# Three of twelve streamed weight blocks loaded in two DMAs each, over 12 and 8 engines

## The chip, the cores and the metric

The kernel runs on one core of a Trainium2 chip (trn2). The metric is the device time in microseconds (us) of one execution. All times are of whole executions of the same program, of which the profile shows one.

## The reference

Two computations share nothing but the output: `a` fills the first 1024 columns, `b` the last 1024. Part A is an attention over 64 segments of 32 rows, one after the other, each with a memory of 8 rows that is the first part of the segment before's output:

```
for s in range(n_seg):                        # 64 segments of 32 rows, Dm = 1024
    h = concatenate([mem, x[s]])              # 8 + 32 rows
    q, k, v = h @ Wq, h @ Wk, h @ Wv          # 32 heads of 128: weights 1024 x 4096 each
    p = softmax(where(mask, q k^T * scale, -1e9))
    o = (p v) @ Wo                            # 4096 x 1024
    mem = o[:, :8]
    outs.append(o[:, 8:])
```

Part B is a state space convolution: a kernel K (from A, B, C and log_dt, 1024 channels of 128 states) is convolved with u over 2048 steps, and `u * Dskip` is added.

## The kernel before, in words

**Order of the stages.** Part B runs first, to about 620 us. In its gaps, part A's weights are loaded and everything of the projections that doesn't depend on the memory is computed ahead and put into DRAM (`PKd`, `VXd`). From about 640 to 1893 us the segment loop of part A runs (`part_a`, the loop over `s` at L406), one segment after the other, since each needs the memory that the one before leaves. A last stage up to 1954 us computes the output rows that were put off (from `OLd`).

**The weights.** Each segment multiplies a small matrix (`a_hT`, 32 columns) by all the weights: 64 blocks of 128 x 2048 bf16, 512 KB each. A block is named by its matrix, half and index, such as (v, 0, 7), here written v07; a block of the output projection by its index, such as o8. 52 blocks stay on the chip all the time, in SBUF and partly in PSUM. Twelve do not fit and are loaded anew in each segment: `STREAM` (L26) and `STREAM_O` (L27) list them. In order of use they are k02, q02, k11, k15, q14, v02, v07, v14, v17, o4, o8, o13.

**How they are streamed.** `streamed_copies` (L63) makes a copy of each of the twelve in DRAM, `WD_...`, of 128 x 2048 in one piece, so that a row is 4096 bytes without a gap. That happens once, during part B. In the loop, `unit` (L300) returns the tile for a block; for a streamed one it calls `stage` (L337), which takes the next of four SBUF slots in turn (`SLOTS = 4`, the tiles `wst` with tags w0 to w3) and issues one DMA on SP's queue (L340). The three first streamed blocks are loaded ahead of the loop (`first`, L1707), and one of the output projection once more behind it (L647).

**What sets the order.** The loop is written under a manual schedule (L290): every engine works through its instructions in the order of the code. A load may start when PE has used the block that was in the slot four loads before; SP waits for that, and what stands behind it on SP waits too. PE uses a block as soon as it has landed: the matmuls of q, k and v are at L414, those of the output projection at L527.

**The other DMAs of a segment** are issued by ACT: `PKd` (L376, 128 KB, the prepared keys), the store to `OLd` (L392), the store of output rows (L396) and the load from `VXd` (L382). GpSimd's copy at L428 waits for `PKd`.

**Semaphores of DMAs.** The DMAs issued by SP and ACT take eight completion semaphores in turn, in the order of the program. A DMA that takes a semaphore waits until the DMA that had it before, eight places back, has landed.

Of the kernel before, what the change touches and what calls it, by code (L numbers as in the profile page):

```python
# [10 lines left out]
BF16 = mybir.dt.bfloat16  # L11
# [13 lines left out]

STREAM = {("k", 0): (2,), ("q", 0): (2,), ("k", 1): (1, 5), ("q", 1): (4,), ("v", 0): (2, 7), ("v", 1): (4, 7)}  # L26
STREAM_O = (4, 8, 13)  # L27

BANK = {("k", 0): "b0", ("q", 0): "b1", ("k", 1): "b2", ("q", 1): "b0", ("v", 0): "b3", ("v", 1): "b2"}
KEPT = {("k", 0, 7): (("K7a", 0, 512), ("K7b", 512, 512), ("K7c", 1024, 512), ("K7d", 1536, 384), (None, 1920, 128)),  # L30
# [28 lines left out]
def streamed_keys():  # L59
    return [key for key in [(m, t, kc) for (m, t), kcs in STREAM.items() for kc in kcs] + [("o", u) for u in STREAM_O]]  # L60


def streamed_copies(ctx, tc, src):  # L63
    nc = tc.nc
    dram = ctx.enter_context(tc.tile_pool(name="a_wd", bufs=1, space=bass.MemoryType.DRAM))
    out, copies = {}, []
    for key in streamed_keys():
        t_ = dram.tile([128, 2048], BF16, name="WD_%s" % "_".join(str(i) for i in key))
        copies.append(lambda t_=t_, key=key: nc.sync.dma_start(
            out=t_[:].rearrange("e (h d) -> e h d", h=2) if key[0] == "o" else t_[:], in_=src(key)))  # L70
        out[key] = t_
    return out, copies


class Ahead:
# [3 lines left out]
    def __init__(self, ctx, tc, x, src, seg_len):  # L79
        self.nc, self.tc, self.x, self.src = tc.nc, tc, x, src  # L80
        self.S, self.Dm = x.shape
        self.SL, self.XM = seg_len, 24
        self.XL, self.KC, self.NS = seg_len - 24, self.Dm // 128, self.S // seg_len
        dram = ctx.enter_context(tc.tile_pool(name="a_dram", bufs=1, space=bass.MemoryType.DRAM))
        self.VXd = dram.tile([self.NS + 1, 128, 256 + self.KC * self.XM], BF16, name="VXd")
        self.PKd = dram.tile([self.NS, 128, 512], BF16, name="PKd")
        self.PVd = [dram.tile([self.NS * self.XL, 2048], BF16, name="PVd%d" % t) for t in range(2)]
        self.OLd = dram.tile([self.NS // 8, 128, 8 * 256], BF16, name="OLd")
# [183 lines left out]
def part_a(ctx, tc, x, src, WD, HE, seg_len, out_a, ahead, W_res, rest, places, first):  # L272
    nc = tc.nc
# [26 lines left out]
    def unit(key):  # L300
        if key in rest:

            rest.remove(key)
            load_resident(tc, wres, src, key, W_res, None, places.pop(0)() if places else None)
        if key in W_res:
            return W_res[key]
        if key in KEPT:
            return ahead_of.pop(key) + halves.get(key, [])
        between.pop(key, lambda: None)()
        if key in first:  # L310
            return first.pop(key)
        if key[0] == "v":
            for k_ in rest[0:3 if key[1] == 0 else 1]:
                rest.remove(k_)
                load_resident(tc, wres, src, k_, W_res)
        return stage(key, WD[key][:])

    ctx_l = ctx_w.enter_context(ExitStack())
    pers = ctx_l.enter_context(tc.tile_pool(name="a_pers", bufs=1))
# [14 lines left out]
    def words(out, in_):  # L334
        nc.vector.tensor_scalar(out=out.bitcast(I32), in0=in_.bitcast(I32), scalar1=0, scalar2=None, op0=ALU.bitwise_or)  # L335

    def stage(key, in_):  # L337
        t_ = wst.tile([128, 2048], BF16, name="wst", tag="w%d" % (loads[0] % SLOTS))
        loads[0] += 1
        nc.sync.dma_start(out=t_[:].rearrange("e (h d) -> e h d", h=2) if len(in_.shape) == 3 else t_[:], in_=in_)  # L340
        return t_

    def load_kept(key):
# [62 lines left out]
    for s in range(NS):  # L406
# [123 lines left out]
        a = quads("k", 0, (0, 2, 4, 6, 1, 3, 5, 7))  # L530
        k0 = evac(a, "k0")
        a = quads("q", 0, range(0, 6))
# [4 lines left out]
        a = quads("k", 1, range(0, 3))  # L537
# [16 lines left out]
        a = quads("q", 1, range(KC))  # L554
# [3 lines left out]
        a = quads("v", 0, range(0, 3))  # L558
# [34 lines left out]
        a = quads("v", 1, range(0, 5))  # L593
# [46 lines left out]
    wo = {}  # L640
    for u in order:
        if ("o", u) in W_res:
            wo[u] = W_res["o", u]
        else:
            wo[u] = spare.pop(0)
            if ("o", u) in WD:
                nc.sync.dma_start(out=wo[u][:], in_=WD["o", u][:])  # L647
            else:
                nc.sync.dma_start(out=wo[u][:].rearrange("e (h d) -> e h d", h=2), in_=src(("o", u)))
    stores(NS - 1, ob)  # L650
# [6 lines left out]
    for b in range(4):  # L657
        pe = [ps_k.tile([128, 512], F32, name="pe", tag="keep%d" % (2 * (b % 2) + n)) for n in range(2)]
        for u in order:
            for hh in range(2):  # L660
                h = 2 * u + hh
                hi = 16 * (h // 16) + 4 * (h % 4) + (h % 16) // 4
# [983 lines left out]
@with_exitstack  # L1646
def kernel(
    ctx: ExitStack,
    tc: tile.TileContext,
    A_x: bass.AP,  # L1650
    A_mem0: bass.AP,
    A_Wq: bass.AP,
    A_Wk: bass.AP,
    A_Wv: bass.AP,
    A_Wo: bass.AP,
    A_seg_len: bass.AP,
    B_u: bass.AP,
    B_A_re: bass.AP,
    B_A_im: bass.AP,
    B_B_re: bass.AP,  # L1660
    B_B_im: bass.AP,
    B_C_re: bass.AP,
    B_C_im: bass.AP,
    B_log_dt: bass.AP,
    B_Dskip: bass.AP,
    out: bass.AP,
):
    seg_len = int(A_seg_len)
    Dm = A_x.shape[2]
    Db = B_u.shape[2]  # L1670
    out_a = out[0, :, 0:Dm]
    out_b = out[0, :, Dm:Dm + Db]
    src = weight_blocks(A_Wq.rearrange("d h e -> d (h e)"), A_Wk.rearrange("d h e -> d (h e)"),
                        A_Wv.rearrange("d h e -> d (h e)"), A_Wo.rearrange("h e d -> (h e) d"))
    WD, copies = streamed_copies(ctx, tc, src)
    ahead = Ahead(ctx, tc, A_x[0], src, seg_len)
    ctx_w = ctx.enter_context(ExitStack())
    W_res, places, first = {}, [], {}
    rest = Keys(RESIDENT)
    rest.ctx = ahead.ctx = ctx_w  # L1680

    def residents(stay, early, uqs, last):
        def put(t_):
            load_resident(tc, None, src, rest.pop(0), W_res, None, t_)
        for _ in range(EARLY[0]):
            load_resident(tc, stay, src, rest.pop(0), W_res)
            yield
        def some(where, tag, n):
            t_ = where.tile([128, n, 2048], BF16, name="W%d" % n, tag=tag)
            return [t_[:, i, :] for i in range(n)]  # L1690
        for t_ in some(stay, "KT1", 2):
            put(t_)
            yield
        for t_ in early:
            put(t_)
            yield
        put(last[0])
        yield
        for t_ in uqs:
            put(t_)  # L1700
            yield
        ahead.wst = ctx_w.enter_context(tc.tile_pool(name="a_wst", bufs=1, side="right"))
        pool = ctx_w.enter_context(tc.tile_pool(name="a_wre0", bufs=1, side="right"))
        for _ in range(EARLY[1]):
            load_resident(tc, pool, src, rest.pop(0), W_res)
            yield
        for i, key in enumerate([("k", 0, 7)] + streamed_keys()[0:SLOTS - 1]):  # L1707
            first[key] = t_ = ahead.wst.tile([128, 2048], BF16, name="wst", tag="w%d" % i)
            tc.nc.sync.dma_start(out=t_[:], in_=WD[key][:] if key in WD else src(key))
            yield  # L1710
        for i in [c // 2 for c in PAIRS]:
            places.append(lambda i=i: stay.tile([128, 2048], BF16, name="W1", tag="MI%d" % i))
        for i in range(LATE):
            put(places.pop(0)())
            yield
        put(last[1])
        yield

    low = low_blocks(ctx, tc)
    ahead.low = low.pop()  # L1720
    copies += [lambda t_=t_: load_resident(tc, None, src, rest.pop(0), W_res, None, t_) for t_ in low]

    def first_state(m0, xt):
        nc = tc.nc
        consts = constants(tc, ahead)
        hT = next(consts)
        nc.sync.dma_start(out=xt[:].rearrange("p k r -> p (k r)"), in_=ahead.VXd[0, :, 256:])
        nc.sync.dma_start(out=m0, in_=A_mem0[0])
        pm = yield
        for kc in range(8):  # L1730
            nc.tensor.transpose(out=pm[:, kc, :], in_=m0[:, kc * 128:(kc + 1) * 128], identity=ahead.consts[0][0:8, 0:8])
        nc.vector.tensor_copy(out=hT[:, :, ahead.XM:], in_=pm)
        nc.gpsimd.tensor_copy(out=hT[:, :, 0:ahead.XM], in_=xt[:])
        yield
        next(consts)
        yield

    with ExitStack() as ctx_b:
        part_b(ctx_b, tc, B_u[0], B_A_re, B_A_im, B_B_re, B_B_im, B_C_re, B_C_im, B_log_dt, B_Dskip, out_b, ahead, copies, residents, first_state)
    with ExitStack() as ctx_a:  # L1740
        part_a(ctx_a, tc, A_x[0], src, WD, A_Wo.shape[0] * A_Wo.shape[1], seg_len, out_a, ahead, W_res, rest, places, first)
# [35 lines left out]
```

## Time and profile before

| what | value |
|---|---|
| runs | 1960.46, 1957.11, 1960.54 us, median 1960.46 us |
| profiled execution: span | 1954.2 us, 2.9 to 6.3 us under the runs |
| PE busy | 1810.2 us (93%) |
| VectorE (DVE) busy | 1379.4 us (71%) |
| ScalarE (ACT) busy | 934.7 us (48%) |
| GpSimd (POOL) busy | 443.1 us (23%) |
| mean granted TensorE clock | 0.974 |
| DMA queue with the most bytes (q1, SP's) | 531.85 MB, 79.9% of 16 engines' span |

The span runs from the first to the last instruction. For the profiled execution no time but the span is given; the runs are timed separately. PE is the matrix engine, PEld its loading of the stationary operand, SPq and ACTq the queues from which SP and ACT issue DMAs. `wst<-WD_v` is a streamed block of v loaded into a slot. A wait line reads: engine, line, what it produces, what it waited for, then the total in us, how often, and the longest.

### The profile page before, as it was taken

Reading aid. Unit: us, or ns where it says so; the run is one execution under the profiler, and the core shown is the slowest. Engines: PE = TensorE matmul, PEld = TensorE weight load, DVE = VectorE, ACT = ScalarE, POOL = GpSimd, SP = SyncE. Lnnn points to the kernel's source line nnn. Section 1 sums busy time; section 2 is a strip of 40 time slices with the busy share of each in tenths; the row PEclk is TensorE's granted clock in tenths of the full one; section 3 lists DMA queues with packets and bytes.
Section 4 is the critical chain, followed back from the end, with each engine's and each line's share of the span. In section 5 each row is a group of like instructions: output and inputs, shape, how many; then the busy total and the mean of one; then the engine's idle time right before and its main releaser. Section 6 shows DMA issues by size and latency. Waiting matters only on the chain.

```text
span 1954.2 us, 74192 instructions
## 1 busy us (share of the span) xinstructions
PE 1810.2 (93%) x31750; PEld 1106.9 (57%) x31788; DVE 1379.4 (71%) x3431; ACT 934.7 (48%) x1670; POOL 443.1 (23%) x855
## 2 busy tenths in 40 slices
PE   8999999887997899999999999999999999998998
PEld 3666666556775555555555555555555555555554
DVE  8599989889994566666676766676766676666650
ACT  8799989851122334344434443444444444444320
POOL 2364545223222111111111111111111111111120
PEclk8999999878998999999999999999999999999999
DMA  7889898867589999999999999999999999999991
GB/s 222 243 232 283 237 287 243 221 188 253 169 272 334 347 340 340 340 339 336 355 339 346 345 335 336 339 341 350 344 350 334 347 341 347 339 350 324 338 343 30
DMA packets 337342, 591.08 MB, mean 302 GB/s; under 512 B 94848, under 2 KB 211048, under 8 KB 334964
## 3 DMA queue, kind: packets, MB, share of 16 engines
q1 hardware_dynamic: 284824, 531.85, 79.9%
q10 hardware_dynamic: 45532, 29.57, 4.9%
q0 software_dynamic: 6656, 24.92, 3.5%
q8 instruction: 249, 4.08, 0.8%
q14 instruction: 81, 0.66, 0.1%
HBM read 528.78 MB, written 68.47 MB: 306 GB/s over the span
## 4 chain that ended last, share of the span: by engine, by line
PE 37%; DMA 27%; DVE 4%; issue 1%; ACT 1%; POOL 0%; SPq 0%; ACTq 0%; DVEq 0%; POOLq 0%
PE acc L414 20%; DMA wst<-WD_v 8%; PE pp L527 8%; DMA wst<-WD_o 7%; DMA wst<-WD_k 3%; DMA arena<-PKd 3%; DMA wst<-WD_q 3%; PE pe L664 3%; PE tr L425 2%; DMA out_dram<-arena 1%; DMA out_dram<-uu 1%; PE pv L495 1%; PE pv L499 1%; DVE arena L621 1%; PE sc L439 1%
## 5 line engine op out<-in xcount | busy, mean ns | idle before, releaser
L414 PEld LDWEIGHTS <-a_hT 128*32 128x32 bf16 x12352 | 328.4, 96 | 324.0 <-issue 64.0
L420 ACT CAST arena<-acc 128x512 bf16<-128x512 f32 x384 | 224.8, 585 | 404.3 <-PE acc L414 324.5
L414 PE MATMUL acc<-wst,a_hT 128*32 128x512 bf16 x2304 | 229.5, 382 | 34.2 <-DMA wst<-WD_v 22.9
L527 PEld LDWEIGHTS <-arena 128*32 128x32 bf16 x8256 | 216.1, 96 | 73.2 <-issue 49.3
L335 DVE TENSOR_SCALAR arena<-keep 128x256 int32<-128x256 int32 (+1 forms) x512 | 175.6, 395 | 28.1 <-PE acc L414 28.0
L428 POOL COPY arena<-arena 128x128 bf16<-128x128 bf16 x128 | 37.3, 292 | 683.0 <-DMA arena<-PKd 314.4
L414 PE MATMUL acc<-XM,a_hT 128*32 128x512 bf16 x2560 | 172.7, 380 | 0.0
L458 ACT ACTIVATE sc<-sc 128x160 f32<-128x160 f32 (+1 forms) x192 | 63.9, 333 | 127.6 <-DVE sc L455 127.6
L454 DVE TENSOR_REDUCE a_mx<-sc 128x4 f32<-128x160 f32 (+1 forms) x192 | 71.7, 374 | 74.7 <-PE sc L442 73.3
L197 PE MATMUL pro<-XM,wsl 128*128 128x512 bf16 x480 | 117.7, 383 | 5.3 <-DVE kst L206 2.2
L527 PE MATMUL pp<-W_o,arena 128*32 128x256 bf16 x3584 | 120.6, 273 | 0.1
L414 PE MATMUL acc<-W,a_hT 128*32 128x512 bf16 x1536 | 120.0, 384 | 0.0
L542 DVE COPY arena<-tr 128x512 bf16<-128x512 bf16 x64 | 27.2, 425 | 128.8 <-PE tr L425 128.8
L462 DVE TENSOR_REDUCE a_mx<-sc 128x4 f32<-128x160 f32 (+1 forms) x192 | 72.9, 379 | 55.3 <-ACT sc L458 54.9
L489 POOL TENSOR_TENSOR arena<-arena,a_BD 128x128 bf16<-128x128 bf16 x128 | 51.1, 399 | 231.1 <-DVE arena L472 229.7
L1266 DVE TENSOR_SCALAR nr<-ptt 128x456 f32<-128x456 int16 x128 | 80.4, 628 | 31.8 <-PE ptt L1244 29.0
L1258 ACT ACTIVATE E<-pa 128x648 bf16<-128x648 f32 x128 | 87.7, 712 | 18.1 <-PE pa L1250 16.0
L414 PE MATMUL acc<-wq,a_hT 128*32 128x512 bf16 x1024 | 92.2, 381 | 0.0
L414 PE MATMUL acc<-g,a_hT 128*32 128x512 bf16 x1024 | 90.4, 379 | 0.0
L1459 POOL TENSOR_TENSOR Bt<-ev 128x512 bf16<-128x512 f32 x32 | 55.7, 1760 | 150.2 <-DVE ev L1456 150.2
L621 ACT CAST arena<-pp 128x128 bf16<-128x128 f32 x64 | 17.0, 265 | 149.8 <-DVE arena L621 149.8
L425 PEld LDWEIGHTS <-arena 128*128 128x128 bf16 x1024 | 57.8, 98 | 54.4 <-issue 45.1
(339 smaller groups left out, 4071.3 us busy)
## 6 DMA issues: line engine op xcount, KB each, us to landing
wst<-WD_v SPq DMA_DIRECT2D x256, 512.0 KB
wst<-WD_k SPq DMA_DIRECT2D x192, 512.0 KB
wst<-WD_o SPq DMA_DIRECT2D x192, 512.0 KB
wst<-WD_q SPq DMA_DIRECT2D x128, 512.0 KB
Ud<-ux POOLq DMA_DIRECT2D x16, 1024.0 KB, 8.2
wq<-Ud SPq DMA_DIRECT2D x32, 512.0 KB
wsl<-in_A_Wk_dram SPq DMA_DIRECT2D x16, 512.0 KB
wsl<-in_A_Wv_dram SPq DMA_DIRECT2D x16, 512.0 KB
```

The source lines that it names most:

```text
L197: nc.tensor.matmul(a[:], lhsT=w[:, kc, 128 * j:128 * j + 128], rhs=xTl[:, kc, :, :].rearrange("p s k -> p (s k)"), start=(kc == 0), stop=( ...
L335: nc.vector.tensor_scalar(out=out.bitcast(I32), in0=in_.bitcast(I32), scalar1=0, scalar2=None, op0=ALU.bitwise_or)
L414: nc.tensor.matmul(a[32 * g:32 * g + 32, o_:o_ + rhs.shape[1]], lhsT=hT[:, kc, :], rhs=rhs, start=(kc == 0), stop=(kc == KC - 1), tile_pos ...
L420: nc.scalar.copy(out=q, in_=a[:])
L425: nc.tensor.transpose(out=p[:, hl, :, :].rearrange("p a b -> p (a b)"), in_=q[:, 128 * hl:128 * hl + 128], identity=ident[:])
L454: nc.vector.tensor_reduce(out=m_, in_=x, axis=AX.X, op=ALU.max)
L458: nc.scalar.activation(out=flat(sc, i), in_=flat(sc, i), func=ACT.Exp, scale=scale)
L462: nc.vector.tensor_reduce(out=m_, in_=x, axis=AX.X, op=ALU.add)
L527: nc.tensor.matmul(po[32 * qt:32 * qt + 32, o_:o_ + rhs.shape[1]], lhsT=oT[:, h % 4, (h % 16) // 4, :], rhs=rhs, start=False, stop=(h == 3 ...
L664: nc.tensor.matmul(pe[n][:], lhsT=left[2 * b + hi // 16][:, 128 * (hi % 16):128 * (hi % 16) + 128], rhs=wo[u][:, 1024 * hh + 512 * n:1024 ...
L1258: sc.activation(out=T["E", r, e // 4][:, lo:lo + 8 * NE].rearrange("p (i c) -> p i c", i=2), in_=T.pop(("p", r, e))[:, :, 0:4 * NE], func= ...
L1266: v.tensor_scalar(out=T["n", r, e // 4][:, lo:lo + 8 * NT], in0=T.pop(("t", r, e))[:, 0:8 * NT].bitcast(I16)[:, 0:16 * NT:2], scalar1=floa ...
```

## The change

The list `PORTIONS` names three of the twelve streamed blocks: k15, v07 and o8. Each is stored in DRAM in two parts and loaded by two DMAs. The first part has 120 rows, stored as 12 stretches of 10 rows; between stretches 64 elements (128 bytes, `PITCH`) are left free, so the 12 stays an outer dimension of the access pattern. The second part has 8 rows, stored as 8 stretches of one row. The slot in SBUF stays one tile of 128 x 2048: rows 0 to 119 come from the first DMA, rows 120 to 127 from the second, which follows it at once on SP's queue. The copies into DRAM are split in the same way. The other nine blocks are loaded as before. A new class `Streamed` holds the parts, makes the copies and issues the loads (in the changed kernel the issue stands at L98).

```diff
@@ -25,6 +25,7 @@
 
 STREAM = {("k", 0): (2,), ("q", 0): (2,), ("k", 1): (1, 5), ("q", 1): (4,), ("v", 0): (2, 7), ("v", 1): (4, 7)}
 STREAM_O = (4, 8, 13)
+PORTIONS = {key: ((120, 12), (8, 8)) for key in (("k", 1, 5), ("v", 0, 7), ("o", 8))}
 
 BANK = {("k", 0): "b0", ("q", 0): "b1", ("k", 1): "b2", ("q", 1): "b0", ("v", 0): "b3", ("v", 1): "b2"}
 KEPT = {("k", 0, 7): (("K7a", 0, 512), ("K7b", 512, 512), ("K7c", 1024, 512), ("K7d", 1536, 384), (None, 1920, 128)),
@@ -60,16 +61,47 @@
     return [key for key in [(m, t, kc) for (m, t), kcs in STREAM.items() for kc in kcs] + [("o", u) for u in STREAM_O]]
 
 
+PITCH = 64
+
+
+class Streamed:
+
+    def __init__(self, dram, nc, src, key):
+        self.nc, self.src, self.key, self.pieces = nc, src, key, []
+        lo = 0
+        for i, (rows, engines) in enumerate(PORTIONS.get(key, ((128, 16),))):
+            name = "WD_%s_%d" % ("_".join(str(j) for j in key), i)
+            each = rows // engines
+            if key in PORTIONS:
+                t_ = dram.tile([engines, each * 2048 + PITCH], BF16, name=name)
+                ap = t_[:, 0:each * 2048].rearrange("a (b f) -> a b f", f=2048)
+            else:
+                ap = dram.tile([128, 2048], BF16, name=name)[:]
+            self.pieces.append((lo, lo + rows, ap))
+            lo += rows
+        assert lo == 128
+
+    def copy(self):
+        for lo, hi, ap in self.pieces:
+            flat = ap if len(ap.shape) == 2 else None
+            w = self.src(self.key)[lo:hi]
+            if self.key[0] == "o":
+                w = w.rearrange("(a b) h d -> a b h d", a=ap.shape[0]) if flat is None else w
+                out = ap.rearrange("a b (h d) -> a b h d", h=2) if flat is None else ap.rearrange("e (h d) -> e h d", h=2)
+            else:
+                w = w.rearrange("(a b) f -> a b f", a=ap.shape[0]) if flat is None else w
+                out = ap
+            self.nc.sync.dma_start(out=out, in_=w)
+
+    def load(self, t_):
+        for lo, hi, ap in self.pieces:
+            self.nc.sync.dma_start(out=t_[lo:hi, :], in_=ap)
+
+
 def streamed_copies(ctx, tc, src):
-    nc = tc.nc
     dram = ctx.enter_context(tc.tile_pool(name="a_wd", bufs=1, space=bass.MemoryType.DRAM))
-    out, copies = {}, []
-    for key in streamed_keys():
-        t_ = dram.tile([128, 2048], BF16, name="WD_%s" % "_".join(str(i) for i in key))
-        copies.append(lambda t_=t_, key=key: nc.sync.dma_start(
-            out=t_[:].rearrange("e (h d) -> e h d", h=2) if key[0] == "o" else t_[:], in_=src(key)))
-        out[key] = t_
-    return out, copies
+    out = {key: Streamed(dram, tc.nc, src, key) for key in streamed_keys()}
+    return out, [w.copy for w in out.values()]
 
 
 class Ahead:
@@ -313,7 +345,7 @@
             for k_ in rest[0:3 if key[1] == 0 else 1]:
                 rest.remove(k_)
                 load_resident(tc, wres, src, k_, W_res)
-        return stage(key, WD[key][:])
+        return stage(key)
 
     ctx_l = ctx_w.enter_context(ExitStack())
     pers = ctx_l.enter_context(tc.tile_pool(name="a_pers", bufs=1))
@@ -334,10 +366,10 @@
     def words(out, in_):
         nc.vector.tensor_scalar(out=out.bitcast(I32), in0=in_.bitcast(I32), scalar1=0, scalar2=None, op0=ALU.bitwise_or)
 
-    def stage(key, in_):
+    def stage(key):
         t_ = wst.tile([128, 2048], BF16, name="wst", tag="w%d" % (loads[0] % SLOTS))
         loads[0] += 1
-        nc.sync.dma_start(out=t_[:].rearrange("e (h d) -> e h d", h=2) if len(in_.shape) == 3 else t_[:], in_=in_)
+        WD[key].load(t_)
         return t_
 
     def load_kept(key):
@@ -644,7 +676,7 @@
         else:
             wo[u] = spare.pop(0)
             if ("o", u) in WD:
-                nc.sync.dma_start(out=wo[u][:], in_=WD["o", u][:])
+                WD["o", u].load(wo[u])
             else:
                 nc.sync.dma_start(out=wo[u][:].rearrange("e (h d) -> e h d", h=2), in_=src(("o", u)))
     stores(NS - 1, ob)
@@ -1706,7 +1738,10 @@
             yield
         for i, key in enumerate([("k", 0, 7)] + streamed_keys()[0:SLOTS - 1]):
             first[key] = t_ = ahead.wst.tile([128, 2048], BF16, name="wst", tag="w%d" % i)
-            tc.nc.sync.dma_start(out=t_[:], in_=WD[key][:] if key in WD else src(key))
+            if key in WD:
+                WD[key].load(t_)
+            else:
+                tc.nc.sync.dma_start(out=t_[:], in_=src(key))
             yield
         for i in [c // 2 for c in PAIRS]:
             places.append(lambda i=i: stay.tile([128, 2048], BF16, name="W1", tag="MI%d" % i))
```

## The prediction

> **What bounds the kernel now.** I began with the page's head and slices, went on to the windows, then to the waits of PE and SP, and last to the timeline of one segment. 0.2% (4 us) is about what a measurement of this kernel can tell from no change.
>
> ```profile
> span 1954.2 us, 74192 instructions
> PE   8999999887997899999999999999999999998998
> DMA  7889898867589999999999999999999999999991
> q1 hardware_dynamic: 284824, 531.85, 79.9%
> q10 hardware_dynamic: 45532, 29.57, 4.9%
> q8 instruction: 249, 4.08, 0.8%
> PE acc L414 20%; DMA wst<-WD_v 8%; PE pp L527 8%; DMA wst<-WD_o 7%; DMA wst<-WD_k 3%; DMA arena<-PKd 3%; DMA wst<-WD_q 3%; PE pe L664 3%; PE tr L425 2%; DMA out_dram<-arena 1%; DMA out_dram<-uu 1%; PE pv L495 1%; PE pv L499 1%; DVE arena L621 1%; PE sc L439 1%
> ```
>
> From slice 13 on, PE and the DMA engines are both at 9 tenths: the segment loop, about 640 to 1893 us. The streamed blocks (WD_) are most of what DMA adds to the chain that ended last. The window of the loop (us, PE, PEld, DVE, ACT and POOL busy, clock, DMA share, GB/s):
>
> ```profile
> 640.00:1893.00 1253.00, 1187.82 (x25440) 693.37 (x25430) 832.09 (x2603) 518.64 (x1140) 200.20 (x510) 1.00 0.96 342
> ```
>
> TensorE has its full clock, PE is busy for 95%, the 16 DMA engines for 96%. A segment lasts 19.60 us (median spacing of PKd's issue). So there is little spare on either side, and what is lost in a segment comes 63 times. What PE waits for in this window (us, times, longest), and SP's and POOL's largest waits:
>
> ```profile
> PE acc L414 <- DMA wst<-WD_v: 16.5, 23, 2.4
> PE pp L527 <- DMA wst<-WD_o: 8.8, 18, 1.3
> PE acc L414 <- DMA wst<-WD_k: 6.4, 11, 1.1
> PE acc L414 <- DMA wst<-WD_q: 4.3, 6, 0.9
> SPq L340 <- PE acc L414: 337.4, 375, 1.6
> POOL arena L428 <- DMA arena<-PKd: 314.4, 48, 8.3
> ```
>
> Only 36.0 us of PE's time goes to late blocks, 0.57 us a segment; SP itself mostly waits for PE to free a slot. One segment's timeline (start, length, what):
>
> ```profile
> 1101.23 0.33 ACTq L376 DMA_DIRECT2D arena<-PKd  x1
> 1101.90 0.62 ACTq L392 DMA_DIRECT2D OLd<-arena  x1
> 1102.56 0.55 ACTq L396 DMA_DIRECT2D out_dram<-arena  x1
> 1106.32 0.32 SPq L340 DMA_DIRECT2D wst<-WD_v  x1
> 1112.14 0.39 PE L414 MATMUL acc<-wst,a_hT 128*32 128x512 bf16 x4
> ```
>
> The fourth line is v07 (block v, 0, 7), the fifth its first use. By the trace's semaphore records PKd landed at 1107.34, OLd at 1108.82, out_dram at 1108.12, v07 at 1111.21, 0.93 us before its use. Over all segments the slack (first use less last landing) has median 0.51 us for v07 (mean 0.53, tenths 0.09 and 0.89), 0.49 (mean 0.54) for k15, 0.31 (mean 0.34) for o8.
>
> **The change, part by part.** Everything is summed against the span, 1954.2 us. The runs shown lie 2.9 to 6.3 us above it, their median 6.3, and that is added at the end.
>
> *Instructions.* PE, DVE, ACT and POOL keep theirs in their order. SP gets 3 more DMAs for the copies, 3 in nearly every one of the 64 segments, and one in the last reload, 196 in all. An issue takes 0.32 us on SP. In the loop these fit into the 337 us and more that SP waits for PE, so I take nothing; uncovered, 192 x 0.32 = 61 us. Ahead of the loop the copies carry the same bytes: 0, within 5 us either way.
>
> *The waits that move (first term).* In the program of both kernels the DMAs of SP and ACT take eight completion semaphores in turn, and each waits until the DMA eight places before it has landed. Before, a segment has 12 on SP and 4 on ACT, 16 in all, so each block always follows the same older DMA: v17 follows PKd, o4 OLd, o13 out_dram, the next k11 VXd, and these had landed 2.5, 3.0, 5.7 and 6.6 us (medians) before the issue. After, there are 19, and the partners move: v07's first piece waits for this segment's PKd, its second piece for OLd, v17 for out_dram, o13 for VXd. In the trace of before, v07 is issued a median 0.91 us before PKd lands and 1.77 us before OLd lands (in 98% and 100% of the segments), v17 0.89 us after out_dram's landing, o13 2.05 us after VXd's. So only v07 is held: its 8-partition piece goes out 1.77 us later. Behind it on SP's queue stand v14 (issued 0.23 us before OLd's landing, so put back by 0.5 with the issues ahead), then v17; v14's wait is in the same stall and is not added. The small piece queues behind the same older packets, so I let it land 1.35 us later than the whole block did. The lower bound is 0.9 (as if only PKd's landing counted), the upper 1.8. Against a slack of 0.53 that scatters, PE stalls 0.85 us a segment (1.35 less 0.53, and a little for the segments that have no slack): 63 x 0.85 = 53 us. The bounds give 63 x (0.9 less 0.53) = 23 and 63 x (1.8 less 0.53) = 80.
>
> *The spread over engines (second term).* A 4096-byte packet takes 159 ns (median) and 180 ns (mean) in 700 to 1850 us. A whole block is 8 packets on each of 16 engines. Split, it is 10 on twelve and one more on eight: 11 on engines 0 to 7, 10 on the next four, none on the last four. That is 3 x 0.18 = 0.54 us later on the busiest engines, if the engine numbers go up from zero; that the first lists really use 12 and 8 engines can be read from stores of these shapes elsewhere in the trace, which land in 12 and 8 parts. For k15 and o8 this takes the slack: with scatter about 0.17 and 0.24 us a segment, 63 x 0.41 = 26 us; between 0 (if the last lander is on an engine that is skipped) and 63 x 1.08 = 68 (no slack at all).
>
> The other nine blocks have to pass engines 0 to 7, which carry 105 packets a segment and not 96, 9 x 0.18 = 1.6 us. With a share of 0.96 they are busy for 18.8 of 19.6 us, so they would need 20.4: a floor of 0.8 us a segment, 63 x 0.8 = 50 us, if packets keep their mean time. This is not added to the stall of v07: both stretch the same segment, and the longer one covers the other. I take half a term on top of the 79, as it bites in bursts: +15, between 0 and 50.
>
> *Relief.* PE stalled at v07 lets v14, v17 and o4, next in line, land in time; their gaps are now 0.16, 0.05 and 0.05 us: 63 x 0.26 = 16, of which I take back 13. The last four engines carry 24 packets less; a quarter of the 36 us of waits, 9 us, could go with them. Sum: 53 + 26 + 15 - 13 - 9 = +72.
>
> *Partitions (third term).* [...] Loads of 8 rows over 8 engines in 295.5 to 301 us had a median packet of 202 ns and not 159 (12 packets); in 305.8 to 313 us they were at 159. So 0 to 11 x 43 ns = 0.47 us for a split block, 0 to 63 x 3 x 0.47 = 89 us if none of it hides. I take 0, since only one of two rows shows it, and keep the end for the range.
>
> [...]
>
> 1954.2 + 72 = 2026, with 6.3 for the runs 2032.
>
> **The rivals.**
>
> *A: the skipped engines were the late ones (faster).* A block's sixteenth landing comes 0.5 to 0.6 us after the fifteenth, the others 0.1 apart. PE's own instruction fetches (q8; 16 KB, 0.92 to 1.06 us, 3.1 in a segment) hold one engine each. If that engine is mostly among the last four, a split block lands 0.5 us sooner, and the 8 packets fewer on each late engine pull the rest along. Price: a gain of 20 to 36 of the 36 us, at worst less 6 for a rest of v07's wait: 1960.5 less 14 to 36 is 1924 to 1946. It decides if most last landings are there and v07's slack absorbs OLd's landing. Against: the packet after a fetch shows a pattern with period 8 over successive fetches, which speaks for a rotation over eight engines, and the slack is 0.53 against 1.35. Chance 0.10.
>
> *B: v07's wait is mostly covered.* A longer segment drains the queues, PKd and OLd land earlier, and the 8-row piece overtakes. Then v07 costs 0.1 to 0.2 us and the spread's 26 us is left, with relief of 9: +25 to +35, 1985 to 1996. For: every lost 0.3 us eases the queue. Chance 0.20.
>
> *C: engines 0 to 7 become the bound.* The floor of 50 us holds, with the partition term on top (a third to all of 89): +80 to +140, 2040 to 2100. For: 0.96 leaves no room. Chance 0.22.
>
> *D: the spread doesn't happen* (the lists merge back into 16 engines). Then only the moved waits stay: 53 less 13, with the relief of none: 2000. The gap of 128 bytes between the parts in DRAM speaks against it. Chance 0.05. No change at all, from terms that cancel: 0.03.
>
> **How the numbers follow.** The forecast of 2032 (its own range 2005 to 2060) has 0.40. With A 0.10, B 0.20, C 0.22, D 0.05 and 0.03 for no change, the range from 1978 to 2100 leaves out A, no change and C's far end. Slower by over 0.2%: 0.87; faster: 0.10; same: 0.03.
>
> **What would show it.** Right: PE's waits for WD_v rise from 16.5 to some 60 us, at v07; SP waits for OLd and PKd at the load's line; segments last 20.6 to 20.8 us; the DMA share of the window falls, as the last four engines idle. For A, segments are under 19.4 us and all four wait rows shrink. For B, WD_v stays under 30 and WD_k and WD_o grow. For C, all rows grow and split blocks' packets are longer than 180 ns. Wrong in its first step, if v07's second piece is issued at once after the first.

## The result, and the profile after

The changed kernel takes 2212.41 us (median of four runs, 2207.93 to 2215.60) and the kernel before 1960.50 us on the same chip: 1.129 times the time, with a 95% interval from 1.126 to 1.131. The change costs 252 us, or 4.0 us in each of 63 segments. The forecast had the sign, with 72 us instead of 252.

From the page of the kernel after: span, the slices of PE and of DMA, the queue of SP, and the chain that ended last.

```profile
span 2212.9 us, 74490 instructions
PE   8999998879867787887887887878778887888789
DMA  7889987685899999989989989999999999998992
q1 hardware_dynamic: 285608, 531.85, 78.2%
DMA wst<-WD_o 15%; DMA wst<-WD_v 14%; DMA wst<-WD_k 9%; PE pp L559 6%; PE acc L446 5%; DMA OLd<-arena 5%; DMA arena<-PKd 4%; PE pe L696 2%; SPq L98 1%; DMA out_dram<-arena 1%; DVE arena L497 1%; DVE arena L503 1%; DVE a_mx L494 1%; DVE arena L545 1%; DMA out_dram<-uu 0%
```

Up to slice 12 the two kernels look alike; in the loop PE falls from 9 to 7 or 8 tenths, while DMA stays at 8 or 9. The bytes of q1 are the same. In the chain, streamed blocks of v, o, k and q were 21% before; now v, o and k alone are 38%. The stretch of the loop that was shown of before (it holds 53 segments of this kernel, and 63 of the kernel before):

```profile
640.00:1893.00 1253.00, 1011.18 (x21100) 581.38 (x21104) 688.49 (x2161) 429.34 (x945) 152.72 (x419) 0.98 0.91 284
```

The engines move 284 GB/s where they moved 342, yet they are busy for 91% of the time (96% before). Some of the share would be the last four engines, which have less to do by the list `PORTIONS` (no trace names an engine). The rest is in the packets: 12% fewer bytes for the same busy time (284 / 0.91 against 342 / 0.96), and the trace's packet records say why. Between 700 and 1850 us a packet of 4096 bytes had a mean of 206.8 ns (180.2 before), and 31% of them were above 200 ns, where before it was 5.6%. The waits of PE, SP and POOL in the stretch 640 to 1893 us of the kernel after:

```profile
PE acc L446 <- DMA wst<-WD_v: 82.5, 63, 7.4
PE acc L446 <- DMA wst<-WD_k: 62.3, 58, 2.2
PE pp L559 <- DMA wst<-WD_o: 55.8, 52, 2.6
SPq L98 <- DMA arena<-PKd: 170.3, 50, 4.8
SPq L98 <- DMA out_dram<-arena: 64.5, 46, 2.4
POOL arena L460 <- DMA arena<-PKd: 452.7, 51, 10.5
```

PE's waits rise on v, k and o together, not at v07 alone, and SP now does wait for PKd where it loads a block. One segment's timeline shows how (the lines of ACT's two DMAs, then SP's issues of v02 and of v07's first part, then PE's first use of v07; in brackets what it waited for):

```profile
1204.40 0.33 ACTq L408 DMA_DIRECT2D arena<-PKd  x1
1205.07 0.33 ACTq L424 DMA_DIRECT2D OLd<-arena  x1
1207.45 0.32 SPq L98 DMA_DIRECT2D wst<-WD_v  x1
1210.48 0.78 SPq L98 DMA_DIRECT2D wst<-WD_v  x1
1217.45 0.40 PE L446 MATMUL acc<-wst,a_hT 128*32 128x512 bf16 x4 [1.34 <-DMA wst<-WD_v]
```

By the trace's semaphore records PKd landed at 1210.40 and OLd at 1211.38; v07's parts were issued at 1210.48 and 1211.40 and landed at 1217.22 and 1217.41. So the two holds of the forecast are there. What it had not priced is that PKd itself takes 6.0 us here (median 6.9 in the loop, 5.5 before). A third hold is there that it had ruled out: v17, one of the `WD_v` issues behind v07, waits for out_dram, which now lands 8.9 us after its issue (5.8 before). In 79% of the segments v17 goes out within 0.1 us behind that landing; in the kernel before, no DMA between 700 and 1850 us follows that closely on the one eight places back. This is SP's line for out_dram above.

### The profile page after: what moved, and what is told of

Same layout as the page of the kernel before. It is cut to its first block, busy times and chain, and to the rows that moved or that the text cites. A ratio compares the mean times of both kernels' runs of the same rounds, so it can differ in the third digit from the quotient of the medians.

```text
span 2212.9 us, 74490 instructions
## 1 busy us (share of the span) xinstructions
PE 1843.6 (83%) x31788; PEld 1113.7 (50%) x31788; DVE 1375.7 (62%) x3431; ACT 935.0 (42%) x1670; POOL 430.3 (19%) x855
## 4 chain that ended last, share of the span: by engine, by line
DMA 49%; PE 17%; DVE 5%; SPq 1%; issue 1%; ACT 1%; ACTq 0%; DVEq 0%; POOL 0%; POOLq 0%
DMA wst<-WD_o 15%; DMA wst<-WD_v 14%; DMA wst<-WD_k 9%; PE pp L559 6%; PE acc L446 5%; DMA OLd<-arena 5%; DMA arena<-PKd 4%; PE pe L696 2%; SPq L98 1%; DMA out_dram<-arena 1%; DVE arena L497 1%; DVE arena L503 1%; DVE a_mx L494 1%; DVE arena L545 1%; DMA out_dram<-uu 0%
## 5 line engine op out<-in xcount | busy, mean ns | idle before, releaser
L446 PEld LDWEIGHTS <-a_hT 128*32 128x32 bf16 x12352 | 323.8, 97 | 510.1 <-DMA wst<-WD_v 120.1
L446 PE MATMUL acc<-wst,a_hT 128*32 128x512 bf16 x2304 | 234.0, 390 | 179.4 <-DMA wst<-WD_v 102.9
L446 PE MATMUL acc<-XM,a_hT 128*32 128x512 bf16 x2560 | 177.5, 388 | 0.0
L559 PE MATMUL pp<-wst,arena 128*32 128x256 bf16 x1536 | 78.1, 277 | 98.5 <-DMA wst<-WD_o 65.2
L229 PE MATMUL pro<-XM,wsl 128*128 128x512 bf16 x512 | 124.4, 387 | 3.2 <-DVE XM L144 1.6
L509 DVE TENSOR_TENSOR arena<-arena,a_BDx 128x512 bf16<-128x512 bf16 x128 | 55.0, 430 | 85.8 <-PE sc L474 63.5
```

Of the source, the lines that this page charges most:

```text
L229: nc.tensor.matmul(a[:], lhsT=w[:, kc, 128 * j:128 * j + 128], rhs=xTl[:, kc, :, :].rearrange("p s k -> p (s k)"), start=(kc == 0), stop=( ...
L446: nc.tensor.matmul(a[32 * g:32 * g + 32, o_:o_ + rhs.shape[1]], lhsT=hT[:, kc, :], rhs=rhs, start=(kc == 0), stop=(kc == KC - 1), tile_pos ...
L509: nc.vector.tensor_tensor(out=out, in0=bc(pt.unsqueeze(2), [128, 4, 4, SL]), in1=bc(BDx[:].unsqueeze(1), [128, 4, 4, SL]), op=ALU.mult)
L559: nc.tensor.matmul(po[32 * qt:32 * qt + 32, o_:o_ + rhs.shape[1]], lhsT=oT[:, h % 4, (h % 16) // 4, :], rhs=rhs, start=False, stop=(h == 3 ...
```

## The experiments

Four causes were open: the rows that an engine writes (whether rows dealt out in another way get in each other's way and make packets longer), the gap in DRAM, the uneven load of the engines, and the moved waits. Times are set against the kernel before on the same chip.

**Single loads.** The kernel before, with loads of different shapes behind its last stage, each waiting for the one before:

```diff
+    probes(ctx, tc, src, oe)     # three rounds of the shapes, into the last output tile
```

> The kernel before, with a row of single loads behind its last stage, one after the other into one tile: 128 rows contiguous; 120 rows on 12 engines with a gap of 128 bytes between the engines' stretches; the same with 4096 bytes; 120 rows contiguous (15 engines); 128 rows on 16 engines with the 128-byte gap; rows 120 to 127 on 8 engines; 96 rows on 12 engines; 64 rows contiguous; 32 rows on 8 engines; rows 0 to 7 on 8 engines. [...] Gap theory (rows that start 128 bytes off in DRAM are slow to read): all shapes with the 128-byte gap at 250 or more, also the 16-engine one and 32 rows on 8; the 4096-byte gap, 120/15 and 64 rows at 159. Load theory (only the number of packets on the first engines counts): every packet at about 159 in every shape. Time about 1954 us and 100 to 150 more for the added loads.

The page's span is 2091.9 us, 138 more than before for the added loads. From the trace's semaphore and packet records, rounds two and three:

| shape | engines | landed, us from issue | median packet, ns |
|---|---|---|---|
| 128 rows contiguous | 16 | 3.1 to 3.3 | 159 |
| 120 rows, 128-byte gap | 12 | 4.5, 4.8 | 166, 194 |
| 120 rows, 4096-byte gap | 12 | 4.9, 4.8 | 159, 193 |
| 120 rows contiguous | 15 | 4.0, 4.0 | 236, 238 |
| 128 rows, 128-byte gap | 16 | 4.4, 4.5 | 226, 233 |
| rows 120 to 127 | 8 | 2.0, 1.9 | 230, 229 |
| 64 rows contiguous | 16 | 3.5, 3.3 | 159, 166 |
| 32 rows, 128-byte gap | 8 | 2.8, 2.9 | 172, 159 |
| 96 rows, 128-byte gap | 12 | 4.6, 4.4 | 211, 189 |
| rows 0 to 7 | 8 | 1.8, 1.8 | 226, 188 |

120 contiguous rows are slow without any gap (236 and 238 ns); a gap of 4096 bytes has 159 and 193 ns where 128 bytes have 166 and 194. All 16 engines with 8 packets each are slow when the rows come in 16 stretches (226 and 233 ns). That speaks for the rows. The shapes with the 128-byte gap stayed under the 250 ns that I had named for a gap (159 to 233), but 64 contiguous rows were near 159, too (159 and 166). The median hides a part of it: above 200 ns are 8 to 19% of the packets of 128 contiguous rows, 28 to 34% of 64 rows, 31 to 41% of 32 rows with the gap, and 55 to 62% of 120 contiguous rows and of the 16 stretches. And 64 rows land no sooner than 128 (3.3 and 3.5 us, against 3.1 to 3.3), with half the bytes.

**The cut alone.** Three blocks in two DMAs each, cut by columns, all engines and partitions as before:

```diff
+        for lo, hi in ((0, 1920), (1920, 2048)) if key in PORTIONS else ((0, 2048),):
...
+            self.nc.sync.dma_start(out=t_[:, lo:hi], in_=ap)
```

> The changed kernel with the same three blocks in two DMAs, but cut by columns: 1920 and 128 of 2048, each over all 128 partitions and 16 engines. 19 DMAs a segment as after; the semaphores' turn holds v07's second piece until PKd has landed (0.9 us after its issue before). [...] Waits theory (the second issue, its hold and what queues behind it on SP make the loss): 2100 to 2200 us.

1961.55 us, ratio 1.001 (0.999 to 1.004). The further issues on SP and 19 DMAs a segment cost nothing, and neither does holding the small second part of v07 for PKd (issued at 5.5 us and not 4.6 after PKd's issue, landed at 10.7 and not 10.3). PE's waits of this kernel, same stretch:

```profile
PE acc L435 <- DMA wst<-WD_v: 23.0, 31, 5.1
PE pp L548 <- DMA wst<-WD_o: 10.8, 19, 2.0
PE acc L435 <- DMA wst<-WD_k: 4.1, 10, 0.9
```

**The twelve engines without the eight.** The second DMAs are gone, and the eight rows of each of the three blocks are left out of the products. 16 DMAs a segment, so no wait moves:

```diff
-PORTIONS = {key: ((120, 12), (8, 8)) for key in (("k", 1, 5), ("v", 0, 7), ("o", 8))}
+PORTIONS = {key: ((120, 12),) for key in (("k", 1, 5), ("v", 0, 7), ("o", 8))}
...
+        return t_[0:120, :] if key in PORTIONS else t_
```

> The changed kernel without the second DMAs: 120 rows over 12 engines with the 128-byte gap, and the 8 rows of the three blocks are left out of the products. 16 DMAs a segment, each with the same partner in the semaphores' turn as before. [...] Waits theory: 1950 to 1975 us. Load theory (two packets more on 12 engines for three blocks, 0.36 us each): 1970 to 2000 us.

2235.86 us, ratio 1.140 (1.136 to 1.145), even more than the change. So the loss is there without the eight-row DMAs and without moved waits; mean packet 207.5 ns, 31% above 200. Why it is slower than the change is open. In its trace the store of output rows lands 9.7 us after issue (5.8 before, 8.9 in the change) and ACT waits for it.

**The gap.** `PITCH = 2048` in place of 64.

> The changed kernel with a gap of 4096 bytes in DRAM in place of 128, so that every row starts on a multiple of 4096 bytes. [...] Gap theory: the packets fall back to 159 to 180 ns and the time to 1980 to 2040 us.

2219.25 us, ratio 1.131 (1.125 to 1.136): the size of the gap is not it.

**Rows without uneven engines.** One DMA a block, 16 stretches of 8 rows:

```diff
+PORTIONS = {key: ((128, 16),) for key in (("k", 1, 5), ("v", 0, 7), ("o", 8))}
```

> The changed kernel with the three blocks in one DMA each: 128 rows as 16 stretches of 8 rows with the 128-byte gap, so 16 engines carry 8 packets each and 16 DMAs a segment wait as before, but each engine writes 8 neighbouring rows (in the row of single loads this shape had a median packet of 226 to 239 ns where the contiguous block had 159). [...] Theory two, uneven engines (only the nine packets more on the first eight count): 1955 to 1970 us.

2192.37 us, ratio 1.119 (1.113 to 1.124): 237 us, far above the 1955 to 1970 us that I had named for uneven engines, with even engines, as many DMAs as before and their waits as before. The mean packet is 216.3 ns, 37% are above 200. The window and PE's waits, 640 to 1893 us:

```profile
640.00:1893.00 1253.00, 1041.70 (x21233) 600.36 (x21232) 689.96 (x2170) 432.94 (x951) 149.33 (x421) 0.97 0.97 286
PE acc L446 <- DMA wst<-WD_v: 66.2, 85, 7.4
PE pp L559 <- DMA wst<-WD_o: 44.0, 62, 2.6
PE acc L446 <- DMA wst<-WD_k: 37.1, 62, 1.8
```

PE waits for all three again. No DMA goes out within 0.1 us behind the one eight places back, as in the kernel before. The DMA share is 0.97, against 0.91 of the change: here all sixteen engines are busy, while the bytes fall to 286 GB/s (284 in the change).

**Halves.** Is it the form of the access pattern rather than the rows? Rows 0 to 63 and 64 to 127, contiguous, and the semaphores in the turn of the change:

```diff
+PORTIONS = {key: ((64, 16), (64, 16)) for key in (("k", 1, 5), ("v", 0, 7), ("o", 8))}
-PITCH = 64
+PITCH = 0
```

> The changed kernel with the three blocks cut into rows 0 to 63 and 64 to 127, each part contiguous in DRAM without a gap and on all 16 engines with 4 packets each: every engine carries 8 packets a block, and 19 DMAs a segment take the semaphores in the turn of the changed kernel, so v07's second part waits for OLd. [...] Theory three, the form of the 16x8 access pattern with its gap is what made it slow, not the rows: 1955 to 2015 us, the upper end being the hold of v07 that I had priced at 53 us.

2234.65 us, ratio 1.144 (1.140 to 1.148). No gap, no odd number of engines, plain rows; mean packet 226.8 ns, 40% above 200, and the engines are busy all the time:

```profile
640.00:1893.00 1253.00, 999.50 (x21028) 576.35 (x21032) 685.01 (x2153) 429.31 (x942) 146.59 (x419) 0.99 1.00 282
```

Cut by columns the same three blocks cost nothing; cut by rows, 279 us. The holds of v07 and v17 are in this run too (its first part follows PKd's landing within 0.1 us in 94% of the segments), so not all of it need be the rows.

**Uneven engines without rows.** The kernel before, with one more DMA over eight engines in each segment, DRAM to DRAM, meant as nine packets of 4096 bytes on each of them:

```diff
+        if key == ("k", 1, 5):
+            nc.sync.dma_start(out=WD["more"][:, 0:9 * 2048].rearrange("a (b f) -> a b f", f=2048),
+                              in_=in_[0:72].rearrange("(a b) f -> a b f", a=8))
```

> The kernel before with one more DMA in each segment, from DRAM to DRAM, of 72 rows over 8 engines, behind the load of k15: nine packets of 4096 bytes more on engines 0 to 7, none on the others, and no load of SBUF changes its shape. Its data is used by nothing. Theory two, uneven engines: 105 packets of 180 ns and 1.3 us of other work need 20.2 us, at 97% 20.8 us a segment, so 2010 to 2050 us, with packets above 200 ns still near 6%. Theory one, which rows an engine writes: 1955 to 1975 us. If both add up to the 252 us of the change, the sum of the two runs' losses shows it.

2045.44 us, ratio 1.045 (1.040 to 1.050): 90 us at a mean 4096-byte packet of 180.5 ns, 6% above 200. The segment is 20.81 us, as expected. But the trace has no nine packets: the DMA went as one packet of 36864 bytes on each of eight engines, 1.51 us long. These come behind k15, ahead of PKd's packets; PKd lands 6.8 us after its issue and not 5.5, and that is where PE waits (same stretch):

```profile
PE sc L443 <- POOL arena L432: 56.8, 48, 2.9
PE acc L418 <- DMA wst<-WD_v: 15.5, 14, 6.1
POOL arena L432 <- DMA arena<-PKd: 433.9, 56, 9.6
```

GpSimd's copy there waits for PKd. The 17th DMA also moves the semaphores' turn: q14, v02, v07 and v14 now go out within 0.1 us behind the landing of the DMA eight places back, in 80 to 100% of the segments, 0.4 to 0.8 us later than before. PE's waits for v did not grow by it (15.5 us, 16.5 before). So this is the price of one long packet ahead of PKd, with moved waits beside it; what nine small packets cost when they are spread over the segment, this run doesn't tell.

**One block.**

```diff
+PORTIONS = {key: ((120, 12), (8, 8)) for key in (("v", 0, 7),)}
```

> The changed kernel with only v07 split, 17 DMAs a segment. Both theories together, priced per packet: 99 packets on the first eight engines at 180 and a third of the 27 ns more, 18.7 us and 1.3 us of other work, at 97% 20.6 us a segment: 2005 to 2040 us. If a split block costs the same wherever there is room or not, a third of 252: 2045 us.

2050.89 us, ratio 1.047 (1.041 to 1.053): 95 us. With 17 DMAs v07's first part isn't held (issued at 4.6 us as before) but lands 7.7 us after its issue and not 5.7, and PE waits there (same stretch):

```profile
PE acc L446 <- DMA wst<-WD_v: 111.0, 102, 7.2
```

**The waits alone.** Cut by columns, with two DMAs of 128 bytes that move the turn so that v07's parts come eight places behind PKd and OLd and v17 behind out_dram, as in the change:

```diff
+        if key == ("v", 0, 7):
+            for i in range(2):
+                nc.sync.dma_start(out=WD["more"][i][:], in_=WD["k", 0, 2].pieces[0][2][0:1, 0:64])
```

> The three blocks cut by columns (1920 and 128 of 2048) over 128 partitions and 16 engines, and two DMAs of 128 bytes from DRAM to DRAM ahead of v07 in each segment, used by nothing. They move the semaphores' turn so that v07's first part waits for PKd, its second for OLd and v17 for out_dram, the same waits as in the change, with no collision of rows and no uneven engines. If the first term of my sum holds, v07 lands about 1.35 us later than before and PE stalls 0.85 us a segment: 2000 to 2035 us. If the segment takes the wait up, as in the cut by columns without the tiny DMAs, with only some 0.3 us for 0.64 us more of issues: 1955 to 1985 us.

2044.32 us, ratio 1.046 (1.041 to 1.050): 91 us. The parts are issued at 5.85 and 6.68 us after PKd's issue and land at 12.0 and 12.2, 1.9 us later than the block did before. Less the slack of 0.53, 63 x 1.36 = 86 us. It is all at v07. But SP's waits (L365 issues the tiny DMAs, L87 the blocks) show that PKd and OLd are seldom what holds it:

```profile
PE acc L440 <- DMA wst<-WD_v: 96.8, 87, 7.6
PE pp L553 <- DMA wst<-WD_o: 6.4, 15, 1.4
SPq L365 <- DMA wst<-WD_k: 65.7, 80, 2.0
SPq L87 <- DMA OLd<-arena: 10.0, 17, 1.3
SPq L87 <- DMA arena<-PKd: 5.9, 8, 1.5
```

The tiny DMAs take their turn too. The second goes out within 0.1 us behind the landing of k15's large part in 98% of the segments, and v07 only 0.6 us behind it, when PKd has landed 0.3 us before. So this run gives the price of a v07 that lands 1.9 us later; what the holds by PKd and OLd cost by themselves in the change, no run tells.

**Two tries at a faster kernel.** The store of a segment's output sits on four engines (in the trace of before its semaphore has four landings behind an early one, where a block's has 16). First, in four DMAs:

```diff
-            nc.scalar.dma_start(out=rows, in_=ob[:, 0, :])
+            for q in range(4):
+                nc.scalar.dma_start(out=rows[q], in_=ob[32 * q:32 * q + 32, 0, :])
```

> The kernel before with the store of a segment's output rows in four DMAs of 32 rows (two rows on each of 16 engines) in place of one whose slowest dimension is 4 and which sits on four engines with 32 packets each. If the busiest engines set the pace, the four are relieved of 24 packets of 27 ns, 0.65 us a segment: 1920 to 1950 us. Against it: three more issues of 0.33 to 0.55 us on ACT, and the semaphores' turn holds the load of VXd until OLd has landed: then 1960 to 2000 us.

2017.62 us, ratio 1.030 (1.025 to 1.035), slower. VXd's issue on ACT is held for OLd, and ACT's casts stand behind it; v02 is held as well (issued 5.5 us after PKd's issue and not 3.1):

```profile
ACT arena L421 <- DMA OLd<-arena: 95.1, 30, 4.7
```

Then stored contiguously by 16 engines and put in order at the end:

```diff
+            nc.scalar.dma_start(out=ahead.OUTd[s], in_=ob[:, 0, :])
...
+            nc.sync.dma_start(out=by_seg[lo:hi, q, 0:XM], in_=from_seg[lo:hi, q, 0:XM])
```

> The kernel before with a segment's output rows stored contiguously in DRAM by 16 engines (8 packets each, in the order of the partitions) in place of by four engines (32 each), and put into the output's order by eight DMAs from DRAM to DRAM in the last stage, where the DMA engines are busy for 27%. As many DMAs in a segment, in the same turn. If the four engines with the extra 24 packets of 27 ns set the pace: 0.65 us a segment less, 1915 to 1945 us, and no more than 10 us given back in the last stage. If they don't: 1950 to 1975 us.

1955.45 us against 1955.54, ratio 1.000 (0.998 to 1.002): the segments shrink by 0.1 us at most, so these four engines don't set the pace. No version was faster than the kernel before.

## Why the prediction was wrong

**The sum of the runs.** What the trace's packet records give, put in one formula: packets on the busiest engine, counted by the list `PORTIONS`, times the mean of all, and 1.4 us of other work (q10 6.1% and q8 1.0% of 19.6 us in the window 700 to 1850 us of before). It is an estimate, since no record names the engine.

| kernel | packets | mean ns | us busy | segment us | busy share |
|---|---|---|---|---|---|
| before | 96 | 180.2 | 18.7 | 19.6 | 0.95 |
| after | 105 | 206.8 | 23.1 | 23.6 | 0.98 |
| 12 engines alone | 102 | 207.5 | 22.6 | 24.1 | 0.93 |
| 16 x 8 rows | 96 | 216.3 | 22.2 | 23.4 | 0.95 |
| halves | 96 | 226.8 | 23.2 | 23.9 | 0.97 |
| one long packet more | 96 and one of 1.51 us | 180.5 | 20.2 | 20.8 | 0.97 |
| only v07 | 99 | 191.0 | 20.3 | 21.0 | 0.97 |
| waits alone | 96 rows (two packets in split blocks) | 189.4 | 19.6 | 21.0 | 0.93 |

In every run the segment is as long as its busiest engines need, to within 7%. So the formula alone doesn't tell which run is bound by its packets: with the waits alone the shapes are those of the cut by columns, and still the mean for a row is 189.4 ns and not 181.4, by the packets of v07 above all (300 to 450 ns on average between 7 and 10 us after PKd's issue). The 16 x 8 run and the one with the twelve engines alone, in which nothing is held, show that packets are longer by the way the rows are cut. Of the 4.4 us that after has more, nine packets at the old mean are 1.6, and 96 packets that are longer by 26.6 ns are 2.6; the rest is the product of both. The holds are not needed for the longer packets: with the twelve engines alone the mean is 207.5 ns without any.

**Third term (partitions): the step that failed.** I took 0, "since only one of two rows shows it", and bounded it with 0.47 us a split block, 89 us. The 16 x 8 run shows 237 us from the way the rows are dealt out alone, with 8 packets on each of 16 engines as before and no hold; it is a neighbour of the change's 10 and 1 rows, not the same. Two things were wrong. Of the two rows, the slow one (202 ns) was the relevant one: loads of 8 rows had 188 to 230 ns alone, too. And I let only the split blocks' own packets grow, by 43 ns; the mean over all of them, unsplit ones included, went from 180 to 216 ns, 96 x 36 ns = 3.5 us on every engine in a segment, where my bound had 1.4. In a loop whose engines were busy for 96% there was 0.8 us to take that up.

In the loop the halves cost 279 us, holds included, where the cut by columns, each DMA over all 128 rows, cost none (1961.55 us, ratio 1.001). But the 16 x 8 run is one DMA a block over all 128 rows and cost 237 us, so how many rows a DMA reaches does not decide alone. No trace names an engine's rows. The runs show that packets get longer with the way the rows are dealt out (a mean of 216.3 ns with 16 x 8 rows and 207.5 with the twelve engines alone, in neither of which anything is held, against 180.2); why they do, no run shows. That the form in 16 stretches is slow by itself is not excluded for this one shape; 120 contiguous rows, alone, were as slow without it (236 and 238 ns, against 226 and 233).

**First term (waits): right in kind, its size open.** The partners moved as said: v07's first part is issued at 6.99 us after PKd's issue, just behind PKd's landing at 6.89, the second at 7.97, behind OLd's at 7.77. Before, the block went out at 4.58, so the parts are 2.4 and 3.4 us later, where the forecast had 0.91 and 1.77: PKd and OLd land later here, because the transfers are slower (PKd lands 6.7 us after its issue in the 16 x 8 run, too, where nothing is held), so the terms feed each other. And "only v07 is held" was wrong, as v17 is held too. I took 53 us, bounds 23 to 80. A v07 that lands 1.9 us later, for another reason, cost 91; what the holds of the change cost by themselves stays open.

**Second term (spread): 26 + 15 taken, its size not measured.** The floor of 50 us was halved without a row for the half. The run that was to measure it had one long packet ahead of PKd in place of nine small ones; it cost 90 us.

**Relief: taken as 22, not seen.** PE's waits for k and o rose to 62 and 56 us instead of falling; only the 4.3 us for q are gone.

**The sum itself.** Rows 237, long packet 90 and late v07 91 make 418; the change cost 252. The last two are not quite the terms of the change, and all three overlap, as I had written for two of them: each stretches the same segment and gives the others room. How the 252 us divide is therefore open; that the rows alone, in the 16 x 8 shape, cost nearly as much is shown.

**The rivals.** C was the nearest: engines 0 to 7 as the bound with longer packets, three of the four wait rows up (v, k and o), but its price of 80 to 140 carried the same short third term. Its sign for itself ("split blocks' packets are longer than 180 ns") held. A is out: nothing was faster, and the run with only the twelve engines lost 275 us. D is out: in the semaphore records of the loop the parts land in 12 and 8 pieces, behind one early event each, and a whole block in 16. B is out, though one piece of it was true: with the column cut, PKd's hold on a small part was covered.

## What to carry to other kernels

Where DMA engines are busy for 96%, cost a new shape of a transfer by what it does to every packet in flight, and test it with the loop's neighbours around it: alone, 64 contiguous rows had the median packet of a full load (159 and 166 ns, against 159), and only the landing time (3.3 and 3.5 us for half the bytes) and the share of packets above 200 ns (28 to 34%, against 8 to 19%) told. Cut a block like these by columns if it has to be cut (ratio 1.001 here), and leave its rows as one plain list of 128: three blocks with all 128 rows in 16 stretches cost 237 us. And where completion semaphores go round, write down for each DMA which older one it now follows, the DMAs of a test included: three DMAs more in a segment were free (ratio 1.001), and five, of which one itself had to wait, cost 91 us. Look in the trace, too, whether a DMA goes as the packets that were meant.

## What I had not expected of the hardware

Cutting 3 of 12 blocks by rows, a quarter of the packets, slows more than that quarter: 37% were above 200 ns with 16 x 8 rows and 40% with halves, against 5.6% before, so packets of unsplit blocks must be among them. And a single load of 128 rows in 16 stretches on 16 engines lands 4.4 to 4.5 us after its issue, where the contiguous one takes 3.1 to 3.3, with the same bytes, packets and engines; 0.4 us of that is a first packet that starts later (1.36 us after the issue, not 0.98).
